# The output's transposes of seven batches: 32 x 32 blocks on VectorE and 128-byte stores in place of TensorE and whole rows

## The chip, the cores and the metric

The kernel runs on one core of a Trainium2 chip. The metric is device time in microseconds, as the median of several runs; smaller is better. A core has five engines that run their own instruction streams in order: TensorE (PE: matmuls and transposes, its weight loads shown as PEld), VectorE (DVE), ScalarE (ACT), GpSimd (POOL) and SyncE (SP), which here only issues DMAs. 16 DMA engines move what the queues give them.

## The reference

```python
# q, k, v: 8 batches x 8 heads x 1152 x 64
q_pool = q.reshape(B, H, S // 2, 2, D).mean(axis=3)
scores = q_pool @ k.T / sqrt(D)                      # 576 x 1152 for each head
attn = softmax(scores); x = attn @ v                 # x: 8 x 576 x 512, heads side by side
theta = x @ w_theta
zr, zi = x * cos(theta), x * sin(theta)
y = einsum('ts,bsd->btd', w_tok_r, zr) + einsum('ts,bsd->btd', w_tok_i, zi)
u = x + y
out = u + maximum(u @ w_ch, 0)                       # 8 x 576 x 512
```

The inputs are spread so that float32 accuracy is needed; each matmul operand is kept as a rounded part (hi) and a rest (lo), and three products are summed.

## The kernel before

The kernel has two stages. The first (to about 885 us) is the attention of 32 pairs of heads; the change leaves it as it is but for one tile's name. The second takes the eight batches one after the other; a list `todo2` of (position, function) is filled with `at2` and then sorted, and this order is that of every engine. A batch has a period of `CYC` = 56 positions, which happen to be about microseconds. The position is counted from the batch's own start, so 58 lies 2 positions into the next batch.

What a batch b does, in order:
- `xload`, `dload`, `xscale` (L242, L223, L237): the attention result x is loaded turned (features on 128 partitions in four quarters c, 576 tokens along the row) and scaled by the reciprocal sums. This runs up to one and a half batches ahead.
- `xhi`, `xlo` (L265, L273): hi and lo of x for theta, on ScalarE and GpSimd.
- `xturn`, `theta` (L281, L291), then `chain` (L302): a transpose of x by TensorE, theta by 12 matmuls into PSUM, and sine, cosine and products by ScalarE, VectorE and GpSimd into the tiles `Z` 0 to 8.
- `token_mix` (L1038): u's sum over tokens on TensorE, in two halves g of 9 steps with 12 matmuls each (L1055). Half 0 fills the feature quarters 0 and 1, half 1 the quarters 2 and 3. Both halves use the same four PSUM banks of the kind "m", so half 1 starts when VectorE has emptied them.
- `uadd` (L1063, instruction L1071): u = x + y from PSUM into the tile `uT`, a quarter at a time. `uT` exists once.
- `uhi`, `ulo` (L1075, L1079; instructions L1077 and L1081): hi and lo of u into two tiles `us0` and `us1`, by ScalarE and VectorE.
- `channel` (L1085, matmuls L1096): u @ w_ch, four output quarters e of 24 matmuls each; `relu` (L1104, L1108): u + max(., 0) in `uT`, by VectorE.
- `oturn`, `ocopy`, `ostore` (L1113, L1125, L1139): the result still has its features on the partitions. For each of five blocks j of 128 tokens (the last of 64) TensorE transposes four 128 x 128 pieces into a PSUM bank (L1119), ScalarE copies them to `on` (L1137), and SP stores rows of 512 floats (L1143). The tokens are kept in an order in which position t * 96 + p is row p * 6 + t of the output; `segments` cuts a block where t changes, which makes nine stores a batch.

The table `OT_AT` says when: blocks 0, 1, 2 at position 58.2, just after the first two steps of the next batch's token mix, and blocks 3 and 4 at 69.55 (65.0 for batch 6), after its half 0. So `uT` can't be written by the next `uadd` before block 4 is transposed. In the last batch the transposes are woven into the end of the channel stage, by a branch of their own.

The loads of one more small table, the softmax sums of batch 7 (`rload`, `recip`, `rsave`), stand at positions 60 to 64 of batch 0.

Of the kernel before, what the change touches and what calls it, by code (L numbers as in the profile page):

```python
# [10 lines left out]
F32 = mybir.dt.float32  # L11
F32R = mybir.dt.float32r
# [3 lines left out]
ALU = mybir.AluOpType  # L16
# [79 lines left out]
)  # L96
CH_AT = (34.7, 41.9, 43.9, 49.7)
RELU_LAG = 2.0
OT_AT = (58.2, 58.21, 58.22, 69.55, 69.56)
OT_AT6 = (58.2, 58.21, 58.22, 65.0, 65.01)  # L100
OT_LAG = (1.0, 1.0, 4.3, 1.0, 1.0)
OT_BANK = "rrtrr"
OT_LAST = "htmmr"
CH_LAST = ("mr", "mr", "mm", "mh")
CH_BANK = "mrmr"
# [10 lines left out]
def pooled_attention_moe_kernel(  # L116
# [11 lines left out]
    nc = tc.nc  # L128
    P = 128
    B, H, S, D = k.shape  # L130
    SQ = S // 2
    DM = H * D
    HALF = SQ // 2
# [3 lines left out]
    QT = 6  # L137
# [3 lines left out]
    ND = DM // P  # L141
# [35 lines left out]
    def bank(kind, name):  # L177
        free = banks[kind]
        free.append(free.pop(0))
        return free[-1]  # L180

    def segments(j):
        a, end = j * P, min((j + 1) * P, SQ)
        while a < end:
            t, p0 = divmod(a, QP)
            n = min(QP - p0, end - a)
            yield slice(a - j * P, a - j * P + n), t, slice(p0, p0 + n)
            a += n
# [8 lines left out]
    bst = {}  # L197
    xTs = []
    pools = {}
# [4 lines left out]
    def width(b):  # L204
        return SQ if b % 2 else 5 * P
# [16 lines left out]

    def dload(b, c):  # L223
        if b == 1:
            if c == 0:
                shape = [P, H // 2, SQ]
                bst[b]["dns"] = pools["up"].tile(shape, F32R, tag="us0", name="dn1", bufs=1)
            dn = bst[b]["dns"][:, c].bitcast(F32)
        else:
            dn = dnp.tile([P, 5 * P], F32, tag="dn", name=f"dn{b}_{c}", bufs=2)  # L230
        bst[b]["dn", c] = dn
        for h in range(2):
            w = width(b)
            src = rd[b][2 * c + h : 2 * c + h + 1, 0:w]
            nc.sync.dma_start(dn[h * D : (h + 1) * D, 0:w], src.broadcast_to([D, w]))
# [145 lines left out]
    def engine(name, b):  # L381
        return getattr(nc, ENG2[name + ("0" if b == 0 else "")])

    with ExitStack() as p1:
# [602 lines left out]
        for c in range(ND):  # L987
            at(X0_AT + X0_DN[c], 13, dload, 0, c)
            at(X0_AT + X0_SC[c], 14, xscale, 0, c, nc.vector)
# [5 lines left out]
        for j in range(AHEAD):  # L995
            t = NU * (NPAIR - 1) + TH_AT[j]
# [15 lines left out]
    with ExitStack() as p2:  # L1012
# [7 lines left out]
        up = pools["up"] = p2.enter_context(tc.tile_pool(name="up", bufs=2))  # L1020
# [6 lines left out]
        def at2(pos, fn, *args):  # L1027
            todo2.append((pos, len(todo2), fn, args))
# [34 lines left out]
        def uadd(b, c):  # L1063
            st = bst[b]
            if c == 0:
                st["u"] = up.tile([P, ND, SQ], F32, tag="uT", name=f"uT{b}", bufs=1)
                for n in range(2):
                    st["us", n] = up.tile([P, ND, SQ], F32R, tag=f"us{n}", name=f"us{n}{b}", bufs=1)
            for u in range(2):
                us = slice(u * HALF, (u + 1) * HALF)  # L1070
                nc.vector.tensor_tensor(  # L1071
                    st["u"][:, c, us], st["xT"][:, c, us], st["py", c, u][:, 0:HALF], ALU.add
                )

        def uhi(b, c):  # L1075
            st = bst[b]
            nc.scalar.copy(st["us", 0][:, c], st["u"][:, c])  # L1077

        def ulo(b, c):  # L1079
            st = bst[b]  # L1080
            engine("ulo", 1).tensor_tensor(  # L1081
                st["us", 1][:, c], st["u"][:, c], st["us", 0][:, c].bitcast(F32), ALU.subtract
            )

        def channel(b, es, half=(0, 1)):  # L1085
            st = bst[b]
            for e in es:
                kinds = CH_BANK[e] * 2 if b < B - 1 else CH_LAST[e]
                pr = st.setdefault(("pr", e), [None, None])
                for u in half:  # L1090
                    pr[u] = bank(kinds[u], f"pr{b}_{e}{u}")
            for k in range(0, 12, 6):
                for e in es:
                    for n, (wi, ui, c) in enumerate(CH_TERMS[k : k + 6]):
                        for u in half:
                            nc.tensor.matmul(  # L1096
                                st["pr", e][u][:, 0:HALF],
                                wch[wi][:, c, e * P : (e + 1) * P],
                                st["us", ui][:, c, u * HALF : (u + 1) * HALF],
                                start=(k + n == 0),  # L1100
                                stop=(k + n == 11),
                            )
# [10 lines left out]
        def oturn(b, j, es=range(ND)):  # L1113
            st = bst[b]
            R = P if j < 4 else HT
            if 0 in es:
                st["po", j] = bank((OT_LAST if b == B - 1 else OT_BANK)[j], f"po{b}_{j}")
            for e in es:
                nc.tensor.transpose(  # L1119
                    out=st["po", j][0:R, e * P : (e + 1) * P],  # L1120
                    in_=st["u"][:, e, j * P : j * P + R],
                    identity=ident,
                )

        def ocopy(b, j):  # L1125
            st = bst[b]
            R = P if j < 4 else HT
            if b < B - 1 or j < 2:
                tag = ("r2b", "xnb")[j % 2]
                on = pools["xe"].tile([P, DM], F32, tag=tag, name=f"on{b}_{j}")  # L1130
            else:
                on = ang.tile([P, DM], F32, tag=("kk", "r2", "xn")[j - 2], name=f"on{b}_{j}", bufs=1)
            st["on", j] = on
            if b == B - 1 and j % 2:
                nc.vector.tensor_copy(on[0:R], st["po", j][0:R])
            else:
                nc.scalar.copy(on[0:R], st["po", j][0:R])  # L1137

        def ostore(b, j):  # L1139
            ov = out[b].rearrange("(p t) e -> t p e", t=QT)  # L1140
            for n, (src, t, ps) in enumerate(segments(j)):
                eng = nc.gpsimd if b == B - 1 and n == 1 else nc.sync
                eng.dma_start(ov[t, ps], bst[b]["on", j][src])  # L1143

        if MAN2:
            p2.enter_context(
# [3 lines left out]
        for b in range(B):  # L1150
            base = CYC * b
            if b > 0:
                if b == B - 1:
                    for n, fn in enumerate((rload, recip, rsave)):
                        at2(60 + 2 * n, fn, b)
                at2(X1_AT if b == 1 else base + PLAN2["xload"], xload, b)
                for c in range(ND):
                    at2(DN1_AT[c] if b == 1 else base + DN_AT[c], dload, b, c)
                    at2(SC1_AT + 0.01 * c if b == 1 else base + SC_AT[c], xscale, b, c, nc.vector)
# [9 lines left out]
            for n, j in enumerate(TURNS[b % 2] if b else TURN0):  # L1169
                t = base + (THETA_AT if b % 2 == 0 else ODD_THETA_AT)[n] if b else THETA0_AT[n]  # L1170
# [12 lines left out]
            for g in range(2):  # L1183
                for i in range(KW):
                    at2(base + TOK_AT[g][i], token_mix, b, g, i)
                for c in (2 * g, 2 * g + 1):
                    t = base + PLAN2[f"uadd{g}"] + 0.7 * (c - 2 * g)
                    at2(t, uadd, b, c)
                    at2(t + 0.7, uhi, b, c)
                    at2(t + 1.4, ulo, b, c)  # L1190
            last = b == B - 1
            for e in range(0 if last else ND):
                at2(base + CH_AT[e], channel, b, (e,))
                at2(base + CH_AT[e] + RELU_LAG, relu, b, e)
            t = base + CH_AT[0]
            for u, es in ((0, (0, 1, 2, 3)), (1, (0, 1)), (1, (2,)), (1, (3,))) if last else ():
# [10 lines left out]
                elif es == (3,):  # L1207
                    for j in js:
                        at2(t + 0.1, oturn, b, j, (0, 1, 2))
                    for j in js:  # L1210
                        at2(t + 1.1, oturn, b, j, (3,))
                        at2(t + 1.2, ocopy, b, j)
                        at2(t + 1.2, ostore, b, j)
            for j in range(0 if last else 5):
                t = base + (OT_AT if b < B - 2 else OT_AT6)[j]
                at2(t, oturn, b, j)
                at2(t + OT_LAG[j], ocopy, b, j)
                at2(t + OT_LAG[j] + 1, ostore, b, j)
        for _, _, fn, args in sorted(todo2, key=lambda e: e[:2]):
            fn(*args)  # L1220

# [29 lines left out]
```

## Time and profile before

| | us |
|---|---|
| median of 3 runs | 1301.83 |
| lowest, highest | 1301.79, 1302.61 |
| span of the profiled execution, first to last instruction | 1299.6 |
| TensorE busy in it | 1285.5 (99%) |
| VectorE busy | 854.9 (66%) |
| ScalarE busy | 710.9 (55%) |
| GpSimd busy | 902.8 (69%) |
| mean share of the 16 DMA engines' time, main queue | 39.2% |

The profile is of one execution. Its span is from the first to the last instruction of the core; the runs' times hold some 2 us more around it. Busy shares are means over two stages that differ: in the second stage GpSimd, ScalarE and the DMA engines have far less to do than these numbers say. TensorE's granted clock was at its full level (2.4 GHz) from end to end (mean 0.999). Times in the rows below are microseconds from the start of the span. The chain of work is followed backwards from the last instruction, at each step to what released it, so a piece on it is one that something later waited for.

### The profile page before, as it was taken

Reading aid. Unit: us, or ns where it says so; the run is one execution under the profiler, and the core shown is the slowest. Engines: PE = TensorE matmul, PEld = TensorE weight load, DVE = VectorE, ACT = ScalarE, POOL = GpSimd, SP = SyncE. Lnnn points to the kernel's source line nnn. Section 1 sums busy time; section 2 is a strip of 40 time slices with the busy share of each in tenths; the row PEclk is TensorE's granted clock in tenths of the full one; section 3 lists DMA queues with packets and bytes.
Section 4 is the critical chain, followed back from the end, with each engine's and each line's share of the span. In section 5 each row is a group of like instructions: output and inputs, shape, how many; then the busy total and the mean of one; then the engine's idle time right before and its main releaser. Section 6 shows DMA issues by size and latency. Waiting matters only on the chain.

```text
span 1299.6 us, 30002 instructions
## 1 busy us (share of the span) xinstructions
PE 1285.5 (99%) x12165; PEld 1069.0 (82%) x12165; DVE 854.9 (66%) x1096; ACT 710.9 (55%) x1260; POOL 902.8 (69%) x669
## 2 busy tenths in 40 slices
PE   8999999999999999999999999999999999999998
PEld 6777777777777777777777777799999999999998
DVE  6677776867777786787778877676455454636432
ACT  4566666566566656656665665655345344435330
POOL 5899999999999999999999998424141324323220
PEclk9999999999999999999999999999999999999999
DMA  7446644644654563466448311223122221213011
GB/s 165 118 109 166 164 110 124 161 137 111 169 141 111 147 168 107 120 171 157 102 119 209 105 47 47 86 74 102 32 92 73 58 64 55 82 37 101 18 37 37
DMA packets 156774, 137.64 MB, mean 106 GB/s; under 512 B 119878, under 2 KB 120268, under 8 KB 156188
## 3 DMA queue, kind: packets, MB, share of 16 engines
q1 hardware_dynamic: 156144, 134.66, 39.2%
q8 instruction: 96, 1.57, 0.6%
q10 hardware_dynamic: 252, 0.60, 0.2%
q0 software_dynamic: 240, 0.46, 0.1%
q14 instruction: 42, 0.34, 0.1%
HBM read 104.96 MB, written 37.94 MB: 110 GB/s over the span
## 4 chain that ended last, share of the span: by engine, by line
PE 94%; DVE 3%; ACT 1%; DMA 1%; issue 0%; ACTq 0%; SPq 0%; POOL 0%; POOLq 0%; DVEq 0%
PE pe L622 25%; PE pa L657 22%; PE pf L1055 16%; PE pf L1096 8%; PE pf L297 7%; PE pm L537 5%; PE pt L492 4%; PE pn L685 2%; PE pf L1119 1%; PE px L554 1%; PE pf L285 1%; DVE mx L544 1%; DMA kn<-in_k_dram 1%; PE pq L297 0%; PE pwt L845 0%; PE pa L577 0%
## 5 line engine op out<-in xcount | busy, mean ns | idle before, releaser
L636 POOL TENSOR_TENSOR ss<-ss,pc 128x576 f32<-128x576 f32 x372 | 543.8, 1462 | 32.0 <-ACT pc L625 6.3
L544 DVE TENSOR_REDUCE mx<-pm 128x2 f32<-128x768 f32 x384 | 358.8, 956 | 167.6 <-PE pm L537 167.4
L625 ACT ACTIVATE pc<-pe 128x576 f32<-128x576 f32 x576 | 348.0, 651 | 52.2 <-PE pe L622 32.0
L657 PE MATMUL pa<-pc,vn 128*64 128x288 f32 x2304 | 294.4, 409 | 0.1
L657 PEld LDWEIGHTS pa<-pc,vn 128*64 128x64 f32 x2304 | 159.5, 137 | 107.0 <-issue 1.8
L374 POOL TENSOR_TENSOR Z<-ab,Z 128x512 fp32r<-128x512 f32 x35 | 46.9, 1341 | 281.2 <-ACT Z L368 237.8
L1055 PE MATMUL pf<-wtk,Z 128*128 128x288 f32 x1728 | 234.6, 295 | 0.8 <-ACT Z L368 0.8
L1055 PEld LDWEIGHTS pf<-wtk,Z 128*128 128x128 f32 x1728 | 230.9, 188 | 2.6 <-ACT Z L368 1.1
L622 PE MATMUL pe<-hi 64*128 64x288 f32 x1152 | 190.4, 327 | 0.9 <-DVE mx L544 0.8
L622 PE MATMUL pe<-nmr,oner 64*128 64x288 f32 x1152 | 170.4, 291 | 0.8 <-DMA nmr<-mT 0.7
L622 PE MATMUL pe<-hi,lo 64*128 64x288 f32 x1152 | 170.2, 291 | 0.0
L622 PE MATMUL pe<-lo,hi 64*128 64x288 f32 x1152 | 170.2, 292 | 0.0
L622 PEld LDWEIGHTS pe<-hi 64*128 64x128 f32 x1152 | 107.9, 184 | 45.3 <-issue 20.0
L537 PE MATMUL pm<-hi 64*128 64x384 f32 x826 | 127.3, 341 | 1.9 <-ACT hi L506 1.7
L669 ACT COPY xu<-pa 128x288 f32<-128x288 f32 x64 | 25.5, 399 | 156.7 <-PE pa L657 120.8
L622 PEld LDWEIGHTS pe<-nmr,oner 64*128 64x128 f32 x1152 | 108.6, 184 | 1.3 <-DMA nmr<-mT 1.3
L622 PEld LDWEIGHTS pe<-lo,hi 64*128 64x128 f32 x1152 | 108.9, 185 | 0.0
L622 PEld LDWEIGHTS pe<-hi,lo 64*128 64x128 f32 x1152 | 108.5, 185 | 0.0
L1096 PE MATMUL pf<-us,wch 128*128 128x288 f32 x768 | 105.4, 296 | 0.0
L1096 PEld LDWEIGHTS pf<-us,wch 128*128 128x128 f32 x768 | 104.0, 189 | 1.6
L636 POOL TENSOR_TENSOR ss<-pc,pc 128x576 f32<-128x576 f32 x62 | 90.9, 1466 | 0.7 <-ACT pc L625 0.7
L537 PEld LDWEIGHTS pm<-hi 64*128 64x128 f32 x826 | 76.5, 184 | 7.3 <-ACT hi L506 1.9
(161 smaller groups left out, 1633.8 us busy)
## 6 DMA issues: line engine op xcount, KB each, us to landing
vn<-in_v_dram SPq DMA_DIRECT2D x32, 576.0 KB
qn<-in_q_dram SPq DMA_DIRECT2D x31, 576.0 KB
kd<-in_k_dram SPq DMA_DIRECT2D x28, 576.0 KB
kn<-kd SPq DMA_DIRECT2D x56, 288.0 KB
xd<-xu SPq DMA_DIRECT2D x32, 288.0 KB
xT<-xd SPq DMA_DIRECT2D x8, 1152.0 KB
qp<-qn SPq DMA_DIRECT2D x56, 144.0 KB
dn<-rd SPq DMA_DIRECT2D x32, 160.0 KB
```

The lines of the kernel that those rows point to most:

```text
L297: nc.tensor.matmul(th, xs[:, c, j * P : (j + 1) * P], ws[:, c], start=(n == 0), stop=(n == 11))
L374: eng.tensor_tensor(Z[1], t, Z[0].bitcast(F32), ALU.subtract)
L492: nc.tensor.transpose(out=dst, in_=src.rearrange("p h d -> p (h d)"), identity=unit)
L537: nc.tensor.matmul(pm[:, h, 0:W], hi[hs, Q0 + j * P : Q0 + (j + 1) * P], hi[hs, K0[3 * g] : K0[3 * g] + W], start=True, stop=True,)
L544: nc.vector.tensor_reduce(mx[:, j : j + 5 : 4, g : g + 1], pm[:, :, 0:W], AX.X, ALU.max)
L622: nc.tensor.matmul(pe[:, h, 0:HALF], w[hs], x[hs], start=(n == 0), stop=(n == 3))
L625: nc.scalar.activation(pcs[u, kt], pe[:, :, 0:HALF], AF.Exp, scale=SC)
L636: nc.gpsimd.tensor_tensor(st["ss", u], first, st["pc"][u, kt], ALU.add)
L657: nc.tensor.matmul(pa[hs, 0, 0:HALF], st["vn"][:, h, kt, :], st["pc"][u, kt][:, h, :], start=(kt == 0), stop=(kt == KT - 1),)
L685: nc.tensor.matmul(px[a : a + 32, 1, 0:HALF], ones, sets[u][n][:, h, :], start=(n == 0), stop=(n == len(sets[0]) - 1), tile_position=(0, a),)
L1055: nc.tensor.matmul(st["py", c, u][:, 0:HALF], Z[zi][:, c * P : (c + 1) * P], wtk[wi][:, kw, u * HALF : (u + 1) * HALF], start=(i == 0 and ...
L1096: nc.tensor.matmul(st["pr", e][u][:, 0:HALF], wch[wi][:, c, e * P : (e + 1) * P], st["us", ui][:, c, u * HALF : (u + 1) * HALF], start=(k ...
```

## The change

For batches 0 to 6 `oturn`, `ocopy` and `ostore` are replaced by `flip` and `fstore`; batch 7 keeps the old way. `flip` is one VectorE transpose for each feature quarter e: it takes the 128 x 576 row of `uT` in 32 x 32 blocks and turns each block in itself. The 32 tokens of a block are taken with a step of three, so that the 32 partitions of a block, after the turn, are each responsible for 18 consecutive rows of the output. `fstore` then writes, for each group of 32 features (g = 0 to 3), 32 partitions x 18 pieces of 32 floats (128 bytes), each to a different row of the output. So a batch has four flips and 16 stores, at the positions 58.0 to 61.1.

The turned tiles `ots` need room. The tiles `us0` and `us1` are cut into halves for it: `us00`, `us01` (hi of quarters 0, 1 and of 2, 3) and `us10`, `us11` (lo). The flips of e = 0, 1 write into `us01`, those of e = 2, 3 into `us11`, when the channel matmuls have read them; the next batch writes them again when its stores have left. The loads `dload` of batch 1 move to `us00` and `us01` likewise.

```diff
-OT_AT = (58.2, 58.21, 58.22, 69.55, 69.56)
-OT_AT6 = (58.2, 58.21, 58.22, 65.0, 65.01)
-OT_LAG = (1.0, 1.0, 4.3, 1.0, 1.0)
-OT_BANK = "rrtrr"
+FLIP_AT = (58.0, 59.0, 60.0, 61.0)
+STORE_LAG = 0.1
...
         def uhi(b, c):
             st = bst[b]
-            nc.scalar.copy(st["us", 0][:, c], st["u"][:, c])
+            if c % 2 == 0:
+                for n in range(2):
+                    st["us", n, c // 2] = up.tile(
+                        [P, 2, SQ], F32R, tag=f"us{n}{c // 2}", name=f"us{n}{b}_{c}", bufs=1
+                    )
+            nc.scalar.copy(st["us", 0, c // 2][:, c % 2], st["u"][:, c])
...
+        def flip(b, e):
+            st = bst[b]
+            if e % 2 == 0:
+                st["ots"] = up.tile([P, 2, SQ], F32, tag=f"us{e // 2}1", name=f"ot{b}_{e}", bufs=1)
+            ot = st["ot", e] = st["ots"][:, e % 2]
+            nc.vector.transpose(
+                out=ot.rearrange("p (n t f) -> p n t f", n=3, t=QT),
+                in_=st["u"][:, e].rearrange("p (t r n) -> p n t r", t=QT, n=3),
+            )
+
+        def fstore(b, e):
+            ot = bst[b]["ot", e].rearrange("p (m f) -> p m f", f=32)
+            ov = out[b].rearrange("(r m) e -> r m e", r=32)
+            for g in range(4):
+                c0 = e * P + 32 * g
+                nc.sync.dma_start(ov[:, :, c0 : c0 + 32], ot[32 * g : 32 * g + 32])
...
-            for j in range(0 if last else 5):
-                t = base + (OT_AT if b < B - 2 else OT_AT6)[j]
-                at2(t, oturn, b, j)
-                at2(t + OT_LAG[j], ocopy, b, j)
-                at2(t + OT_LAG[j] + 1, ostore, b, j)
+            for e in range(0 if last else ND):
+                at2(base + FLIP_AT[e], flip, b, e)
+                at2(base + FLIP_AT[e] + STORE_LAG, fstore, b, e)
```

How the instruction streams stand. TensorE where batch 2's token mix ends its first half, before (pf are PSUM banks, wtk the token weights, Z the products, wth the theta weights, ident the identity matrix; L1119 is the transpose of the output):

```order
L1055 MATMUL pf_12646<-wtk_82,Z_8_13784 128x288 x2
L1055 MATMUL pf_12646<-wtk_81,Z_8_13785 128x288 x2
L1119 MATMUL pf_12648<-ident,uT_13537 128x128 x4
L1119 MATMUL pf_12648<-ident,uT_13537 64x128 x4
L285 MATMUL pf_12647<-ident,xT_12662 128x128 x4
L297 MATMUL pf_12647<-wth_79,xh_14053 128x512 x4
L297 MATMUL pf_12647<-wth_79,xl_14054 128x512 x4
```

and after (line numbers of the changed file differ a little):

```order
L1054 MATMUL pf_12646<-wtk_82,Z_8_13772 128x288 x2
L1054 MATMUL pf_12646<-wtk_81,Z_8_13773 128x288 x2
L284 MATMUL pf_12647<-ident,xT_12662 128x128 x4
L296 MATMUL pf_12647<-wth_79,xh_14043 128x512 x4
L296 MATMUL pf_12647<-wth_79,xl_14044 128x512 x4
```

The eight transposes between the token mix and the next transposes of x are gone; the twelve at position 58.2 are gone in the same way, and nothing else changes place on TensorE.

VectorE at the same place, before (xT is the input that `xscale` scales, L1071 is `uadd`, L1081 `ulo`):

```order
L343 TENSOR_TENSOR ti<-xn,ti 128x512
L240 TENSOR_TENSOR xT_12662<-xT_12662,dn_2_13884 128x576
L240 TENSOR_TENSOR xT_12662<-xT_12662,dn_3_13892 128x576
L1071 TENSOR_TENSOR uT_14143<-xT_10577,pf_12649 128x288 x2
L1071 TENSOR_TENSOR uT_14143<-xT_10577,pf_12646 128x288 x2
L1081 TENSOR_TENSOR us_14145<-uT_14143,us_14144 128x576
```

and after:

```order
L342 TENSOR_TENSOR ti<-xn,ti 128x512
L239 TENSOR_TENSOR xT_12662<-xT_12662,dn_2_13872 128x576
L239 TENSOR_TENSOR xT_12662<-xT_12662,dn_3_13880 128x576
L1155 STREAM_TRANSPOSE ot_0_13973<-uT_13526 128x576 x2
L1155 STREAM_TRANSPOSE ot_2_14008<-uT_13526 128x576 x2
L1068 TENSOR_TENSOR uT_14117<-xT_10577,pf_12649 128x288 x2
L1068 TENSOR_TENSOR uT_14117<-xT_10577,pf_12646 128x288 x2
```

The four flips stand between the scaling of the next input and the addition of the token mix's first half.

SP's DMA queue after batches 0 and 1, after the change (ot are the turned tiles, rc, rf and rd the small tables of sums, xd and xT the next inputs, dn their broadcast sums):

```order
L1165 DMA out_dram<-ot_0_13376 576x1x32 x8
L208 DMA rc_13413<-sd_100 128x36
L1165 DMA out_dram<-ot_2_13411 576x1x32 x8
L215 DMA rf_148<-rc_13413 128x36
L217 DMA rd_140<-rf_148 8x576
L219 DMA rd_139<-rf_148 8x64
L354 DMA odd<-kk 64x512
L355 DMA ab<-ti 64x512
L245 DMA xT_12662<-xd_88 128x4x576
```

Where nine stores of rows stood (rc ahead of them, rf and rd between them), there are now two groups of eight, with rc between them and rf and rd behind them; the next input load follows as before.

## Rows read from the trace of the kernel before

**Rows 1.** The page: span, TensorE's busy time, and the chain's shares by engine.

```profile
span 1299.6 us, 30002 instructions
PE 1285.5 (99%) x12165; PEld 1069.0 (82%) x12165; DVE 854.9 (66%) x1096; ACT 710.9 (55%) x1260; POOL 902.8 (69%) x669
...
PE 94%; DVE 3%; ACT 1%; DMA 1%; issue 0%; ACTq 0%; SPq 0%; POOL 0%; POOLq 0%; DVEq 0%
```

**Rows 2.** The chain in order of time: start, length, engine, tile, line, count.

```profile
902.93 1.31 PE pf L1119 x12
...
915.36 0.87 PE pf L1119 x8
...
1031.46 0.87 PE pf L1119 x8
1032.33 0.44 PE pf L285 x4
1032.77 2.77 PE pf L297 x12
...
1080.05 11.11 PE pf L1055 x84
1091.17 0.87 PE pf L1119 x8
...
1115.97 3.17 PE pf L1096 x24
...
1251.38 1.31 PE pf L1119 x12
...
1262.21 0.87 PE pf L1119 x8
```

**Rows 3.** Timeline of VectorE: start, length, instruction, count, idle before and releaser.

```profile
1019.69 1.67 DVE L240 TENSOR_TENSOR xT<-xT,dn 128x640 f32<-128x640 f32 x1 [0.16 <-DMA dn<-rd]
1032.37 1.55 DVE L1071 TENSOR_TENSOR uT<-xT,pf 128x288 f32<-128x288 f32 x4 [11.01 <-PE pf L1119]
1034.08 0.76 DVE L1081 TENSOR_TENSOR us<-uT,us 128x576 fp32r<-128x576 f32 x1 [0.16 <-ACT us L1077]
...
1080.16 2.52 DVE L240 TENSOR_TENSOR xT<-xT,dn 128x576 f32<-128x576 f32 x2
1092.08 1.55 DVE L1071 TENSOR_TENSOR uT<-xT,pf 128x288 f32<-128x288 f32 x4 [9.40 <-PE pf L1119]
```

**Rows 4.** VectorE by line and shape: count, busy us, mean ns, idle before.

```profile
L648 DVE TENSOR_TENSOR sv_l<-sv_l,pc 128x576 f32<-128x576 f32 x2 | 3.6, 1802 | 0.2
```

**Rows 5.** Lines L458 and L1143 on SP: ns least, median, most; landing us.

```profile
L458 SPq DMA_DIRECT2D qp<-qn x56: 613/656/1707, 74.0 to 754.8; - x56
...
DMA to landing us min/median/max: 3.0/3.5/4.3
```

**Rows 6.** DMA view of 6 to 9 us, then of 767.4 to 768 us.

```profile
DMA packets 2587, 0.65 MB, mean 218 GB/s; under 512 B 2587, under 2 KB 2587, under 8 KB 2587
...
q1 hardware_dynamic: 144, 0.02, 19.8%
```

**Rows 7.** Timeline of VectorE, the third and fourth quarter of the subtraction.

```profile
1114.31 2.49 DVE L1081 TENSOR_TENSOR us<-uT,us 128x576 fp32r<-128x576 f32 x2
```

**Rows 8.** The DMA queue's own waits: us in total, times, the longest.

```profile
SPq L219 <- DMA rf<-rc: 14.7, 8, 2.6
```

**Rows 9.** Timeline of GpSimd, after two batches.

```profile
1017.57 1.28 POOL L374 TENSOR_TENSOR Z<-ti,Z 128x512 fp32r<-128x512 f32 x1
1018.82 1.86 POOL L374 TENSOR_TENSOR Z<-odd,Z 128x512 fp32r<-128x512 f32 x1
1021.78 6.14 POOL L276 TENSOR_TENSOR xl<-xT,xh 128x640 fp32r<-128x640 f32 x4 [1.10 <-issue]
...
1082.02 1.81 POOL L374 TENSOR_TENSOR Z<-ti,Z 128x512 fp32r<-128x512 f32 x1
```

More of the change, by code (lines that the diff above doesn't have):

```diff
@@ L224, in dload @@
         if b == 1:
[L225 to L228, printed above, removed]
+            if c % 2 == 0:
+                bst[b]["dns"] = pools["up"].tile(
+                    [P, 2, SQ], F32R, tag=f"us0{c // 2}", name=f"dn1_{c}", bufs=1
+                )
+            dn = bst[b]["dns"][:, c % 2].bitcast(F32)
         else:
@@ L1066, in uadd @@
                 st["u"] = up.tile([P, ND, SQ], F32, tag="uT", name=f"uT{b}", bufs=1)
-                for n in range(2):
-                    st["us", n] = up.tile([P, ND, SQ], F32R, tag=f"us{n}", name=f"us{n}{b}", bufs=1)
             for u in range(2):
@@ L1076, in uhi @@
             st = bst[b]
-            nc.scalar.copy(st["us", 0][:, c], st["u"][:, c])
+            if c % 2 == 0:
+                for n in range(2):
[3 more added lines that the diff above has]
+            nc.scalar.copy(st["us", 0, c // 2][:, c % 2], st["u"][:, c])
         def ulo(b, c):
@@ L1081, in ulo @@
             engine("ulo", 1).tensor_tensor(
-                st["us", 1][:, c], st["u"][:, c], st["us", 0][:, c].bitcast(F32), ALU.subtract
+                st["us", 1, c // 2][:, c % 2],
+                st["u"][:, c],
+                st["us", 0, c // 2][:, c % 2].bitcast(F32),
+                ALU.subtract,
             )
@@ L1098, in channel @@
                                 wch[wi][:, c, e * P : (e + 1) * P],
-                                st["us", ui][:, c, u * HALF : (u + 1) * HALF],
+                                st["us", ui, c // 2][:, c % 2, u * HALF : (u + 1) * HALF],
                                 start=(k + n == 0),
@@ L1116, in oturn @@
             if 0 in es:
-                st["po", j] = bank((OT_LAST if b == B - 1 else OT_BANK)[j], f"po{b}_{j}")
+                st["po", j] = bank(OT_LAST[j], f"po{b}_{j}")
             for e in es:
@@ L1127, in ocopy @@
             R = P if j < 4 else HT
-            if b < B - 1 or j < 2:
+            if j < 2:
                 tag = ("r2b", "xnb")[j % 2]
@@ L1133, in ocopy @@
             st["on", j] = on
-            if b == B - 1 and j % 2:
+            if j % 2:
                 nc.vector.tensor_copy(on[0:R], st["po", j][0:R])
@@ L1141, in ostore @@
             for n, (src, t, ps) in enumerate(segments(j)):
-                eng = nc.gpsimd if b == B - 1 and n == 1 else nc.sync
+                eng = nc.gpsimd if n == 1 else nc.sync
                 eng.dma_start(ov[t, ps], bst[b]["on", j][src])
+        def flip(b, e):
[6 more added lines that the diff above has]
+                in_=st["u"][:, e].rearrange("p (t r n) -> p n t r", t=QT, n=3),
+            )
+        def fstore(b, e):
[4 more added lines that the diff above has]
+                nc.sync.dma_start(ov[:, :, c0 : c0 + 32], ot[32 * g : 32 * g + 32])
         if MAN2:
```

## The prediction

> **What bounds the kernel now.** I read the page first: TensorE is busy for 99% of the span, and the chain of work that ended last lies on TensorE for 94% [rows 1]. So a microsecond taken from TensorE shortens the run, unless the next wait takes it back. Next I read that chain in order of time over the second part of the kernel (from about 885 us on), where the eight batches of the expert stage follow each other, one every 56 us. It has no gap: each piece begins where the one before it ends, and twice in a batch the piece is L1119, the transposes of the output [rows 2]. After that I read the timelines of VectorE, GpSimd and the DMA queue at the two places where these transposes stand, to see who has room for the work that takes their place.
>
> The DVE timeline shows the place that matters most: between the last L240 (scaling the next batch's input) and the next L1071 (adding the first half of the token mix), VectorE has nothing to do for about ten microseconds in each batch [rows 3].
>
> **What is removed.** Per batch the chain holds 12 transposes in 1.31 us and 8 in 0.87 us, together 2.18 us [rows 2]. That they are on the path is plain from the view: the token-mix matmuls before them and after them touch them. The change drops both groups for batches 0 to 6; the first pair is the one at 902.93 and 915.36, the last the one at 1251.38 and 1262.21. The sum is 7 x 2.18 = **15.26 us**. Batch 7 keeps its own. With them go 35 ScalarE copies of the result out of PSUM and 63 of the large stores. ScalarE is not on the path, so I count nothing for it.
>
> **What is added on VectorE.** Four flips per batch, each 128 x 576 floats with one input. No row shows this operation. Its bounds: 0.76 us, what L1081 takes for the same 576 columns with nothing beside it [rows 3], and 1.80 us, what an addition of 576 columns takes with GpSimd at work beside it [rows 4]. I take 0.8, since a flip has one SBUF input and not two, and keep 1.80 for the range. So a batch gets 3.0 to 7.2 us.
>
> The room for it: in one kind of batch VectorE is free from 1019.69 + 1.67 = 1021.36, in the other from 1080.16 + 2.52 = 1082.68 [rows 3]. The first half of the token mix ends 1.31 us sooner than now: in the second kind at 1091.17 - 1.31 = 1089.86. TensorE then has its four input transposes and twelve theta matmuls, 0.44 + 2.77 us, before it needs the PSUM banks that L1071 empties in 1.55 us [rows 2, 3]. So the flips may last until 1089.86 + 3.21 - 1.55 = 1091.5, which is 8.8 us or 2.2 us each (10.4 us in the first kind). Even 7.2 fits. The flips cost nothing on the path.
>
> The Trainium skill speaks against this step: "VectorE: DVE Perf Modes", under Rules for kernel authors, gives a 128 x 128 transpose to TensorE where PSUM will do as a destination. Its table of the three transpose paths has 311 ns for 128 columns of bf16 on VectorE; an estimate from that is 576/128 x 0.311 = 1.4 us a flip, 5.6 us a batch. By it the sum would be the same, since 5.6 is below 8.8; by the rule taken alone the step would be a loss, but the rows have TensorE full and VectorE with room.
>
> **What is added on the DMA queue.** Instead of nine stores a batch there are 16, each of 32 partitions x 18 pieces of 128 bytes: 576 pieces, 36 for each of 16 DMA engines. Two costs. Issue: the nearest row is the move of qp, also 576 pieces, 0.656 us on the queue [rows 5]; 16 x 0.656 = 10.5 us. Moving: pieces of 256 bytes loaded from DRAM went at 218 GB/s, so 256 x 16 / 218 = 18.8 ns a piece and engine; 128 writes of 144 bytes to DRAM (with 16 four-byte marks) held 19.8% of 16 engines for 0.6 us, so 0.198 x 600 x 16 / 144 = 13.2 ns [rows 6]. A store then needs 0.5 to 0.7 us of each engine, about the issue time, so no backlog builds up.
>
> Who waits for them: the flipped tiles lie in the second halves of the operand pair us, so the next batch's ScalarE copy (L1077, third quarter) and VectorE subtraction (L1081, third quarter) must wait until the stores have read them. In the tighter kind of batch the first store can go at 1082.68 + 0.76 = 1083.44, the last is issued by 1093.9 and, with the 3.5 us that a store takes to land [rows 5], is done at 1097.4. The subtractions start at 1114.31 [rows 7], 1112.1 after the shift of 2.18. That leaves 14.7 us. The cover is gone when a store takes (1112.1 - 3.5 - 1083.44)/16 = 1.57 us, which is 44 ns a piece. Behind the stores on the queue stand the next input load and its broadcasts; they now wait for the second L1071 of the batch, so 10 us of stores in front of them cost nothing. In batch 0 a small load of sums stands between the stores, and a reciprocal waits for it on VectorE ahead of L1071: at most 2.6 us, the longest such wait [rows 8], once, against about 1.6 us that TensorE leaves; I count 0, and 1 us for the range.
>
> **What comes closer.** All other producers keep their pace while TensorE reaches its reads 1.31 us (later 2.18 us) sooner. The nearest: GpSimd finishes the low part of Z7 at 1082.02 + 1.81 = 1083.83 [rows 9], and TensorE reads it after 56 of the 84 matmuls of that piece, now at 1080.05 + 7.4, after the change at 1086.1 [rows 2]. 2.3 us are left. The low parts xl are done at 1021.78 + 6.14 = 1027.92 [rows 9]; theta reads the last quarter at 1031.46 - 1.31 + 0.44 + 7 x 0.23 = 1032.2, so 4.3 us are left.
>
> **The sum.** 1299.6 us of span in the profiled execution, less 15.26, is 1284.3. The median of the runs, 1301.83, is 2.2 us above that span; I carry these over: **1286.6 us**.
>
> **The rivals.**
> 1. *The stores become the bound.* Each batch waits for the 128-byte pieces of the one before. It decides from 44 ns a piece. Speaking for it: no row shows thousands of small writes to DRAM in a row; the 13.2 ns are from 128 of them. Against: neither the 18.8 ns nor the 13.2 ns come near. At four times 18.8 ns a store takes 2.7 us, 16 take 43.3, and they are done at 1083.44 + 43.3 + 3.5 = 1130.2. TensorE itself waits from about 1116 on (its first 16 matmuls of the channel stage don't need that quarter, and they start at 1115.97 - 2.18 [rows 2]; the subtraction takes 1.25 more), so the subtraction is 15.6 us late for its last start at 1114.6. Seven times: 109 us, **1396 us**, slower. The Trainium skill, "DMA: Bandwidth & Descriptors", Specifications, says that pieces below 512 bytes are read, modified and written. The trace of the 144-byte writes does not show it; if each piece were moved twice the price would be 37 ns, still under the point, but near enough that this rival gets some chance.
> 2. *GpSimd loses to the flips what TensorE gains.* GpSimd works on xl while the flips run. A GpSimd instruction that lay beside a VectorE one took 1.86 us in place of 1.28 [rows 9]. Four times that excess is 2.3 us, inside the 4.3. If GpSimd stood still for four flips of 1.80 us, xl would be 7.2 - 4.3 = 2.9 us late in each batch: 20.3 us against the 15.26, **1307 us**. At 1.6 us a flip gain and loss cancel: 1301.
> 3. *Part of it comes back.* One of the short rooms above (2.3 us to Z7, 1.6 us to the emptied banks, the load in batch 0) is overrun by up to a microsecond or so a batch: **1289 to 1299 us**.
>
> **How the numbers follow.** Chance of the forecast (1285 to 1288): 0.72. Of rival 3: 0.12. Of rival 1: 0.09. Of rival 2: 0.07, of which 0.04 ends within 0.2%. A measurement of this kernel can tell 0.2%, some 2.6 us, from no change. So faster 0.72 + 0.12 = 0.84, same 0.04, slower 0.12. The range takes the forecast and the greater part of rival 3: 1285 to 1296.
>
> **What would show it.** Right: L1119 has 20 transposes left; the chain in order of time still has no gap, and its period is 2.18 us shorter; flips take 0.7 to 1.0 us; the last 128-byte store of a batch is issued 11 to 13 us after its first flip; no ScalarE or VectorE wait at the copy and subtraction names an output DMA. Wrong: a wait of L1077 or L1081 for out (rival 1), stores on the queue of over 1.5 us each; TensorE idle before the theta matmuls, released by GpSimd (rival 2), or before the second half of the token mix, released by VectorE (flips over 2.2 us).

## The result, and the profile after

| | before | after |
|---|---|---|
| median of the runs, us | 1301.81 | 1286.62 |
| lowest to highest, us | 1301.73 to 1302.61 | 1286.24 to 1289.90 |
| span of the profiled execution, us | 1299.6 | 1285.2 |
| VectorE busy, us | 854.9 | 882.4 |
| ScalarE busy, us | 710.9 | 694.2 |

The ratio is 0.9889, 95% interval 0.9875 to 0.9903. The median fell by 15.2 us; 15.26 were forecast. That the median meets the forecast of 1286.6 to a few hundredths is partly luck, since single runs lie between 1286.24 and 1289.90.

The page of after, to be held against [rows 1]: the span, the busy time of each engine, and the chain's shares.

```profile
span 1285.2 us, 29776 instructions
PE 1271.3 (99%) x12025; PEld 1054.7 (82%) x12025; DVE 882.4 (69%) x1124; ACT 694.2 (54%) x1225; POOL 905.1 (70%) x669
...
PE 91%; POOL 3%; DVE 3%; ACT 1%; DMA 1%; issue 1%; ACTq 0%; POOLq 0%; SPq 0%; DVEq 0%
```

TensorE has 140 matmuls fewer, 20 for each of seven batches, and is still busy for 99%. VectorE took on 27.5 us, and no wait for it shows on TensorE. The 3% that GpSimd has of the chain are L635 in the first stage, which the change leaves alone. The chain of after in order of time (start, length, engine, tile, line, count) shows what became of the place of [rows 2]:

```profile
1012.68 14.28 PE pf L1054 x108
1026.96 0.44 PE pf L284 x4
1027.40 2.80 PE pf L296 x12
1030.20 7.93 PE pf L1054 x60
...
1070.22 14.28 PE pf L1054 x108
...
1274.35 0.87 PE pf L1124 x8
```

Where twelve transposes cut the first half of the token mix into 24 and 84 matmuls, 108 now follow each other; the eight behind them are gone too. From one first half to the next it is 1070.22 - 1012.68 = 57.54 us; before, from one group of eight transposes to the next in the same two batches, it was 1091.17 - 1031.46 = 59.71 [rows 2], so the period is 2.17 us shorter. L1124, the old way, stands in batch 7 alone. That there is no gap is told in one line by the busy times from 887 to 1260 us, PE first, the granted clock and the DMA engines' share near the end:

```profile
887.00:1260.00 373.00, 373.00 (x2582) 357.72 (x2581) 221.98 (x365) 153.07 (x253) 117.46 (x83) 1.00 0.28 64
```

TensorE is busy for all 373 of 373 us. VectorE's timeline at the two places of [rows 3] (start, length, instruction, count, idle before and what ended it):

```profile
1018.13 3.52 DVE L1155 STREAM_TRANSPOSE ot<-uT 128x576 f32<-128x576 f32 x4
1026.20 1.61 DVE L1068 TENSOR_TENSOR uT<-xT,pf 128x288 f32<-128x288 f32 x4 [4.54 <-PE pf L1054]
...
1077.27 3.53 DVE L1155 STREAM_TRANSPOSE ot<-uT 128x576 f32<-128x576 f32 x4
1083.74 1.62 DVE L1068 TENSOR_TENSOR uT<-xT,pf 128x288 f32<-128x288 f32 x4 [2.94 <-PE pf L1054]
...
1106.78 2.50 DVE L1083 TENSOR_TENSOR us<-uT,us 128x576 fp32r<-128x576 f32 x2
```

The four flips fill the space that was idle; VectorE still waits 4.5 and 2.9 us for TensorE behind them, not the other way about. The last row is the subtraction of [rows 7]: no idle time in front of it, so no store held it. The same view of all 32 subtractions, and of all 32 copies of L1079, names no output DMA.

### The profile page after: what moved, and what is told of

Read it like the earlier page. It is cut to its first block, busy times and chain, and to the rows that moved or that the text cites. A ratio compares the mean times of both kernels' runs of the same rounds, so it can differ in the third digit from the quotient of the medians.

```text
span 1285.2 us, 29776 instructions
## 1 busy us (share of the span) xinstructions
PE 1271.3 (99%) x12025; PEld 1054.7 (82%) x12025; DVE 882.4 (69%) x1124; ACT 694.2 (54%) x1225; POOL 905.1 (70%) x669
## 4 chain that ended last, share of the span: by engine, by line
PE 91%; POOL 3%; DVE 3%; ACT 1%; DMA 1%; issue 1%; ACTq 0%; POOLq 0%; SPq 0%; DVEq 0%
PE pe L621 24%; PE pa L656 21%; PE pf L1054 17%; PE pf L1101 8%; PE pf L296 7%; PE pm L536 5%; PE pt L491 3%; POOL ss L635 3%; PE pn L684 2%; PE px L553 1%; PE pf L284 1%; DVE mx L543 1%; DMA kn<-in_k_dram 1%; PE pq L296 0%; ACT pc L624 0%
## 5 line engine op out<-in xcount | busy, mean ns | idle before, releaser
L635 POOL TENSOR_TENSOR ss<-ss,pc 128x576 f32<-128x576 f32 x372 | 544.1, 1463 | 32.0 <-ACT pc L624 6.2
L635 POOL TENSOR_TENSOR ss<-pc,pc 128x576 f32<-128x576 f32 x62 | 90.9, 1466 | 0.7 <-ACT pc L624 0.7
```

The costliest lines, as they stand in the source:

```text
L635: nc.gpsimd.tensor_tensor(st["ss", u], first, st["pc"][u, kt], ALU.add)
```

## The experiments

Each differs from the kernel after by the lines shown; a negative sign is a line of the kernel after.

**e1: the work that was added, taken out.**

```diff
-            for e in range(0 if last else ND):
-                at2(base + FLIP_AT[e], flip, b, e)
-                at2(base + FLIP_AT[e] + STORE_LAG, fstore, b, e)
```

> The changed kernel without any flip and any store for batches 0 to 6 (their output is left out, batch 7 is whole). Theory (the gain is TensorE's 15.26 us, and flips and stores lie wholly in time that was idle): same as the changed kernel, 1286 to 1287.5 us. Rival (flips and stores take something of the gain back): faster than the changed kernel by what they cost, 1 us or more, since no batch waits for them.

Measured: 1286.12 us (1286.01 to 1286.16), ratio to before 0.9880 [0.9866, 0.9895]. Without any flip and any store of batches 0 to 6 the kernel is 0.5 us shorter, with intervals that overlap. So flips and stores together cost at most that; the run of after whose mean granted clock was 1.000 took 1286.24 us, 0.1 above.

**e2: all 140 transposes put back beside the flips.** `oturn` is scheduled again at its old positions, into the old banks (their tables are put back too, not shown).

```diff
...
+            for j in range(5):
+                if not last:
+                    at2(base + (OT_AT if b < B - 2 else OT_AT6)[j], oturn, b, j)
```

> The changed kernel with the 140 TensorE transposes put back at their old places, their results unused: no copies to SBUF and no stores of rows; flips and 128-byte stores stay. Theory (the gain is TensorE time alone): 1286.6 + 7 x 2.18 = 1301.9 us, the time of before. Rival (the gain comes from the 35 ScalarE copies or the lighter row stores that went): well below, 1287 to 1295.

Measured: 1301.42 us (1301.14 to 1302.29), ratio 0.9999 [0.9990, 1.0009]. The whole gain is gone. The chain of e2, in order of time:

```profile
1019.10 1.31 PE pf L1127 x12
1020.41 11.11 PE pf L1057 x84
1031.53 0.87 PE pf L1127 x8
```

They stand with the lengths of [rows 2], 1.31 and 0.87 us. The ScalarE copies and the old stores were not put back, and the time of before is reached without them: taking them out was worth nothing that shows.

**e3: only the twelve of each batch put back** (`range(3)` in the line above).

> The same with the first 12 transposes of each batch alone (1.31 us), not the 8 after the first half of the token mix. Theory: 1286.6 + 7 x 1.31 = 1295.8 us; the two groups add. Rival (the eight that stood before the next batch's addition were the costly ones, since that addition had to wait for them): less than 1290.

Measured: 1295.21 us (1295.18 to 1296.01), ratio 0.9952 [0.9936, 0.9969]. 7 x 1.31 = 9.2 were due over 1286.62, that is 1295.8; 8.6 came. Gain and transposes go together, piece by piece.

**e4: the flips' source read side by side, not with a step of three.** The rows of the output then stand in another order.

```diff
-                in_=st["u"][:, e].rearrange("p (t r n) -> p n t r", t=QT, n=3),
+                in_=st["u"][:, e].rearrange("p (n t r) -> p n t r", t=QT, n=3),
```

> The flips read their 32 columns side by side and not with a step of three (the order of the output's rows is wrong by that for batches 0 to 6). If the step makes a flip take 0.94 us in place of the 0.8 that I forecast: 0.75 to 0.80 us a flip here. If the transpose itself does: 0.9 to 0.95. The time stays at 1286 to 1287.5 either way.

A single run: 1286.05 us. The flip's line in after, and then in e4 (count, least, median and most ns, first and last start):

```profile
L1155 DVE STREAM_TRANSPOSE ot<-uT x28: 918/944/976, 906.4 to 1239.6; 128x576 f32<-128x576 f32 x28
```

```profile
L1155 DVE STREAM_TRANSPOSE ot<-uT x28: 728/731/770, 905.1 to 1237.8; 128x576 f32<-128x576 f32 x28
```

The step of three costs 0.21 us a flip, 0.85 us a batch, all of it in time that VectorE has to spare.

**e5 and e6: each flip done twice, and four times.**

```diff
+            for _ in range(2):
                 nc.vector.transpose(
...
```

For e6 the 2 is a 4, for e9 further below a 3.

> Every flip is done twice in place (8 a batch). After the change four flips take 3.53 us and VectorE then still waits 2.94 us in the tighter kind of batch, and 2.4 us more may pass before TensorE needs the banks. Theory (room of 8.8 us a batch): 2 x 3.53 = 7.06 us fits, 1286 to 1287.5 us. Rival (the flips are hidden by luck, with no room left): 7 x 3.5 us more, 1311.

Measured: 1287.10 us (1286.28 to 1287.29), ratio 0.9884 [0.9868, 0.9901]. 7.5 us of flips in a batch cost nothing that stands out from the runs' spread, and in the second stage of the profile no wait of TensorE shows.

> Every flip four times: 14.1 us a batch. Theory: over the room by 5.3 us in the three batches of the tighter kind (flips from 1077.27 to 1091.4, the addition should begin by 1086.1), by 3.6 to 3.9 in the three of the other kind, nothing in the last, where the second half of the token mix uses other banks: 27 us, 1313 us, with TensorE idle before the second half of the token mix, released by VectorE's addition. Rival (GpSimd is held back by flips, so that the low parts for theta come late): TensorE idle before theta instead, and xl's four subtractions well over 5 to 7 us.

Measured: 1331.53 us (1330.91 to 1332.11), ratio 1.0227 [1.0212, 1.0243]: the wait came, but with a loss of 45 us over the kernel after in place of some 26. The expected 1313 us was missed by 18. Timeline of TensorE in e6, two of the six batches in which it waits:

```profile
988.35 10.14 PE L1054 MATMUL pf<-wtk,Z 128*128 128x288 f32 x60 [5.83 <-DVE uT L1068]
1049.09 10.45 PE L1054 MATMUL pf<-wtk,Z 128*128 128x288 f32 x60 [4.31 <-DVE uT L1068]
```

The waits are those that the theory names, 30.4 us in six where 27 were expected. But the 60 matmuls behind each, 7.93 us in the chain of after, take 10.1 and 10.5. (A row of the timeline is 0.16 us longer than the same piece of the chain, and the wait in front of it is that much shorter, so that the two together add up.) Busy times and granted clock around the second of the two (the clock is the third number from the end):

```profile
1044.80:1049.10 4.30, 0.01 (x1) 0.01 (x1) 4.09 (x7) 0.00 (x0) 0.00 (x0) 0.75 0.43 69
1049.10:1052.60 3.50, 3.50 (x13) 3.27 (x14) 3.33 (x7) 2.40 (x4) 0.00 (x0) 0.50 0.53 84
1052.60:1056.00 3.40, 3.40 (x23) 3.40 (x23) 1.40 (x3) 1.77 (x3) 0.00 (x0) 0.82 0.00 0
1056.00:1059.50 3.50, 3.50 (x29) 3.50 (x28) 0.70 (x2) 1.22 (x2) 2.54 (x2) 1.00 0.00 0
```

In the stretch in which TensorE stood idle the granted clock fell to its half level (1.2 GHz); it was still there when the matmuls came back, 13 of them in 3.5 us where 29 go at the full level, and rose to 2.4 GHz in the course of the next stretch. Over the six batches the 60 matmuls took 61.65 us where 6 x 7.93 = 47.58 would do: 14.1 us on top of the 30.4, 44.5 together, against the 44.9 by which the median is above the kernel after.

**e7 and e8: each store done twice, and three times** (the further ones into scratch tensors). The small load of sums of batch 0 stands ahead of the stores in both.

```diff
...
                 nc.sync.dma_start(ov[:, :, c0 : c0 + 32], ot[32 * g : 32 * g + 32])
+                for n in range(1):
+                    xv = xo[n][b].rearrange("(r m) e -> r m e", r=32)
+                    nc.sync.dma_start(xv[:, :, c0 : c0 + 32], ot[32 * g : 32 * g + 32])
...
```

For e8 the 1 is a 2.

> Every 128-byte store is sent twice, the second time to a scratch tensor in DRAM (32 stores a batch; the small load of sums in batch 0 is put ahead of them). Stores now go at 0.67 to 0.73 us each and move at 12.6 ns a piece. Theory (room for 1.57 us a store): 32 x 0.7 = 22.4 us and 2 to 3 us to land fit into the 28.5 us between first store and the subtraction that waits: 1286 to 1287.5 us. Rival (writes of 128 bytes to DRAM run into a limit of the memory that 16 stores in a burst don't show): stores over 1 us each, and 1290 or more.

Measured: 1287.03 us (1286.27 to 1287.59), ratio 0.9885 [0.9871, 0.9900]. 32 stores in a row of 0.63 us each stay hidden: in the second stage of the profile no wait of TensorE shows.

> Every store three times, 48 a batch, two of them to scratch tensors. Theory: 48 x 0.7 = 33.6 us and about 2.5 to land end some 4.5 us after the last moment at which the subtraction of the third quarter may start; seven batches, 31 us: 1310 to 1325 us, with VectorE's subtraction L1083 waiting for an output DMA. Rival (another queue entry behind the stores, the next input load or the small tables, waits longer and is what ends last): the wait is named at the scaling or at theta, not at the subtraction.

Measured: 1332.19 us (1328.92 to 1335.39), ratio 1.0232 [1.0213, 1.0252]. The direction is as expected, the size is 7 us beyond the range that was named. The waits of e8, of VectorE and then of TensorE (us in total, times, the longest):

```profile
DVE us L1084 <- DMA xo<-ot: 38.4, 6, 8.8
```

```profile
PE pf L1102 <- DVE us L1084: 27.5, 7, 7.0
```

The seventh of VectorE's waits, 4.5 us in batch 0, the profile puts down to a small load (rf from rc) that stands behind the stores and landed last; it too is named at the subtraction.

The chain of e8 in order of time, and the busy times with the granted clock (third number from the end) of two stretches of it:

```profile
1063.49 0.63 SPq L1169
1064.16 2.25 DMA xo<-ot
...
1066.54 0.77 DVE us L1084
1067.35 2.48 PE pf L1102 x8
1069.83 1.05 PE pf L285 x4
```

```profile
1060.00:1067.00 7.00, 4.48 (x27) 3.79 (x25) 2.57 (x6) 1.94 (x3) 0.00 (x0) 1.00 0.72 122
1067.00:1070.40 3.40, 3.05 (x11) 2.58 (x12) 3.23 (x7) 1.13 (x3) 0.09 (x1) 0.56 0.90 265
```

This is the mechanism of the prediction's first rival: the last store is issued, lands, frees the half tile, the subtraction runs, and TensorE behind it. And again the matmuls behind the wait are slow: eight of the channel stage take 2.48 us where 24 take 3.20 in the chain of after, and four transposes 1.05 where they take 0.44, at a granted clock of 0.56. Here the clock did not fall while TensorE stood still (from 1064.48 to 1067.35 us): to 1067.00 it was at its full level, and it was low when the matmuls had come back. Added up like this behind all seven waits (2.9 to 7.0 us long), it is 2.1 to 3.4 us each and 18.5 in all; with the 27.5 of the waits 46.0, where the median is 45.6 above the kernel after.

**e9: each flip done three times,** to find from which wait on the clock falls.

> Each flip is done three times over, 12 in a row on VectorE, some 11.5 us a batch. With 16 in a row, in the six batches that wait, the flips took 15.4 us and TensorE waited 4.31 us in one kind of batch and 5.83 us in the other, so the room is about 11.1 and 9.5 us. Theory A (what the flips lack in room is all that is lost): waits of 0.4 us in three batches and 2.0 us in three, 7 us in all, about 1294 us. Theory B (after each such wait the granted clock falls to half as it did with 16 flips, where the 60 matmuls behind the wait took 2.0 to 2.9 us more): another 3 x 2.3 us if only the longer waits do it, about 1301, or 6 x 2.3, about 1308.

Measured: 1299.92 us (1298.05 to 1301.18), ratio 0.9984 [0.9975, 0.9994]. TensorE's timeline, the first two of the six batches, and the last:

```profile
918.07 0.53 PE L1054 MATMUL pf<-wtk,Z 128*128 128x288 f32 x2 [0.44 <-DVE uT L1068]
918.80 7.93 PE L1054 MATMUL pf<-wtk,Z 128*128 128x288 f32 x58 [0.20 <-DVE uT L1068]
978.40 0.53 PE L1054 MATMUL pf<-wtk,Z 128*128 128x288 f32 x2 [1.99 <-DVE uT L1068]
979.13 9.47 PE L1054 MATMUL pf<-wtk,Z 128*128 128x288 f32 x58 [0.20 <-DVE uT L1068]
...
1212.59 0.53 PE L1054 MATMUL pf<-wtk,Z 128*128 128x288 f32 x2 [1.99 <-DVE uT L1068]
1213.32 7.92 PE L1054 MATMUL pf<-wtk,Z 128*128 128x288 f32 x58 [0.19 <-DVE uT L1068]
```

The waits are the 0.4 and 2.0 us that were worked out. Behind the three waits of 0.4 us the clock stayed; behind 2.0 us it fell in two batches out of three (9.47 here, 9.29 in the fourth) and stayed in the last of them. The busy times and the granted clock (third number from the end) around the first wait of 1.99 us:

```profile
976.40:978.40 2.00, 0.02 (x1) 0.00 (x0) 1.86 (x5) 0.00 (x0) 0.00 (x0) 1.00 0.68 109
978.40:982.00 3.60, 3.40 (x16) 3.17 (x17) 3.43 (x7) 2.41 (x4) 0.00 (x0) 0.71 0.53 85
```

While TensorE stood still the clock was at its full level (1.00); it fell behind the wait (0.71 in the mean of that stretch). Behind the last wait it was 1.00 throughout.

Theory A named the waits and missed the rest. Theory B's time (1301) is nearest, but it is right in part only: the clock cost 1.54 + 1.36 = 2.9 us where 7 were allowed, and something that neither named took more. After any wait two matmuls start, and the next 58 wait once more for the second pair of L1068's additions: 0.53 + 0.20 us, while the 58 then take 7.93 us, as much as 60 in the chain of after. That is 0.73 us a batch, 4.4 in six. The sum: 6 x 0.73 + 3 x 0.43 + 3 x 1.99 + 2.9 = 14.5. The profiled execution has a span 13.9 us longer than that of after and began its second part 0.8 us sooner, so 14.7 were to be explained.

## Why the prediction was right, point by point

**What is removed.** Right in mechanism and size: 7 x 2.18 us. e2 gives all of it back, e3 the part of the twelve. The profiled execution's span is 0.9 us above the 1284.3 of the sum. That lies ahead of the change: the transposes of x below are those of the same place in the two traces, before and then after, and the second part begins 1.1 us later there. In that execution the granted clock over the first 50 us was 0.97 of the full level, where before has 1.00; e5's, with 0.97 as well, begins its second part as late (888.25). e1, e4 and e7, which leave TensorE's work as it is in after, have 1.00 there and spans of 1284.3, 1284.0 and 1284.2.

```profile
886.96 0.44 PE pf L285 x4
```

```profile
888.10 0.44 PE pf L284 x4
```

**The flips.** The term was a little small: 0.944 us at the median where 0.8 was taken, inside the bounds and inside the 0.7 to 1.0 that the text set for itself. e4 shows the reason: 0.73 us is the price side by side, near the 0.76 of [rows 3], and the step of three in the source is the rest. The Trainium skill's table of three transpose paths ("VectorE: DVE Perf Modes") led to an estimate of 1.4 us, which the trace does not bear out. The rule of the Trainium skill that the prediction set against this step (same page, Rules for kernel authors) gives a 128 x 128 transpose to TensorE where PSUM will do as a destination. A flip is not such a transpose: it turns 32 x 32 blocks, each in itself, and the addresses of the stores do the rest. So the rule did not speak against the step, as the prediction had it. What the way by TensorE costs here is the 15 us of e2, since TensorE is the engine without room.

The room for the flips was put at 8.8 us in one kind of batch and 10.4 in the other. e6 measures it: 15.35 us of flips less a wait of 5.83 is 9.5, and 15.39 less 4.31 is 11.1. Both are 0.7 us more than forecast, because the sum let TensorE wait for all of L1071's 1.55 us; e9's rows show that the first matmuls start after half of them. e5 (7.5 us, no wait that shows) and e9 (11.5 us, waits in both kinds) lie on the two sides.

**The stores.** Right: issued in 0.63 us each (0.656 forecast), the last one issued 12.7 and 11.8 us after the first flip began (11 to 13 forecast), and 13.1 in batch 0, where the small load stands between them. The SP queue of after in batch 0 and in these two batches:

```profile
907.38 6.03 SPq L1165 DMA_DIRECT2D out_dram<-ot  x8
913.46 0.62 SPq L208 DMA_DIRECT2D rc<-sd  x1
...
1019.13 11.67 SPq L1165 DMA_DIRECT2D out_dram<-ot  x16
...
1078.28 10.77 SPq L1165 DMA_DIRECT2D out_dram<-ot  x16
```

The point from which rival 1 decides, 1.57 us for a store's turn, was sound as well: e7 makes it 2 x 0.67 = 1.35 (stores follow each other every 0.67 us) and nothing waits, e8 makes it 2.0 and the subtraction waits. In e8's chain it is the issues on SP that follow each other; the pieces are quicker. The DMA view of after from 1076.5 to 1092 us, packets, megabytes and share of 16 engines:

```profile
q1 hardware_dynamic: 9472, 1.18, 47.7%
```

0.477 x 15.5 us x 16 / 9472 = 12.5 ns a piece (16 x 576 of them, and 16 marks a store), under the 13.2 to 18.8 that were taken. The Trainium skill, "DMA: Bandwidth & Descriptors" (Specifications), has pieces below 512 bytes read, modified and written; no run here shows a price for it: the pieces of 128 and of 144 bytes both lie below 512, and whatever it costs is inside their 12.5 and 13.2 ns.

**Batch 0's reciprocal.** Here the step was wrong, without harm. "At most 2.6 us" was the longest wait of another load [rows 8] and left out that the load now stands behind eight stores on its own queue, the 6.03 us above. VectorE's timeline:

```profile
915.49 0.38 DVE L212 RECIPROCAL rc<-rc 128x36 f32<-128x36 f32 x1 [5.59 <-DMA rc<-sd]
915.79 1.48 DVE L1068 TENSOR_TENSOR uT<-xT,pf 128x288 f32<-128x288 f32 x4
```

The chain of after at that place, from the end of the first half:

```profile
915.21 0.44 PE pf L284 x4
...
918.45 7.93 PE pf L1054 x60
```

The wait was 5.6 us. It was hidden because L1068 could not have started before 915.21, when TensorE ended its half: 0.6 us were lost of what VectorE had, and L1068 ended at 917.27, 1.2 us before TensorE's next matmul of the token mix at 918.45. An estimate from these rows: two stores more ahead of the load, at 0.67 us each, would use that up. e5 bears it out: there the doubled flips put off the stores, the load and with them the reciprocal to 916.90, 1.4 us later, and the same 60 matmuls took 8.10 us, 0.17 more.

**GpSimd.** Rival 2 fell: xl of the tighter kind of batch, before (no flip beside it) and after (a flip beside it for 2.3 us, from 1078.47 to 1080.80):

```profile
1083.80 5.03 POOL L276 TENSOR_TENSOR xl<-xT,xh 128x512 fp32r<-128x512 f32 x4
```

```profile
1076.69 1.82 POOL L373 TENSOR_TENSOR Z<-ti,Z 128x512 fp32r<-128x512 f32 x1
1078.47 5.06 POOL L275 TENSOR_TENSOR xl<-xT,xh 128x512 fp32r<-128x512 f32 x4
```

In the other kind of batch the four subtractions took 6.75 us where [rows 9] have 6.14. Here are the rows of after, with flips beside them, and of e1, without any:

```profile
1017.48 6.75 POOL L275 TENSOR_TENSOR xl<-xT,xh 128x640 fp32r<-128x640 f32 x4
```

```profile
1016.62 6.71 POOL L275 TENSOR_TENSOR xl<-xT,xh 128x640 fp32r<-128x640 f32 x4
```

e1 has the same time without flips, so the 0.6 us are not theirs: in both kernels xl now starts earlier and beside the scaling of the input (L239). The flips did not hold GpSimd back. The Z7 row of after, the first of the pair above, ends at 1078.51; TensorE reads Z7's low part after 80 of the 108 matmuls that start at 1070.22, at 1080.8: the 2.3 us that were forecast are there.

**What was wrong in the rivals' prices.** Rival 1 worked with waits alone. The runs that drove the kernel into such a wait (e6, e8) lost about half as much again and more (14 us on 30, 18 on 27), because the granted clock falls during the wait or behind it and part of the next matmuls runs at half speed. The forecast itself did not touch this, since no wait arose.

## What to carry to other kernels

When TensorE is busy without a gap, a transpose that another engine can do in its idle time is worth its TensorE time, whatever it costs there; find out how long that engine may take, not how fast it is. The same view says how much more can be put in: here one more flip for each, or one more store for each, cost nothing that stood out, and the next step lost nearly all or more than all of the gain. A wait put on a TensorE that has had none is to be priced above its length.

## What the runs showed of the hardware

- **A wait of TensorE costs more than it lasts.** In the profiled executions the granted clock stayed at its full level behind waits of 0.43 us (three of three, e9), fell to half behind 1.99 us in two of three, and did so with all thirteen waits from 2.9 us up (e6, e8). It fell during the longer waits of e6, but behind the wait in e9, and in the stretch of e8 above no sooner than its last moment. The matmuls after it then lost 1.4 to 1.5 us (e9) and, the restart included, 2.0 to 3.4 us (e6, e8); the restart with its second short wait alone cost 0.73 us (e9). Why one of the waits of 1.99 us left the clock alone is open: the rows show nothing that differs between the three. Over e9's ten runs the mean granted clock lies between 0.996 (the longest span, 1299.4 us) and 0.999 (the shortest, 1296.3), so how often it fell seems to differ from run to run.
- **A 32 x 32 block transpose of 128 x 576 floats** takes 0.73 us from adjacent columns and 0.94 us with a step of three in the source, about the 0.76 us of a subtraction of that size. GpSimd's four subtractions took 6.75 us with such transposes beside them and 6.71 without (after, e1).
- **Writes of 128 bytes to DRAM** took 12.5 ns of a DMA engine each, and a store of 576 of them 0.63 us on the issuing queue, with 16 or 32 in a row and for most of 48.
